# Routing splits and comparisons moved from VectorE to GpSimd, with new dates, in a clustered-attention and MLP kernel

## The chip, the cores and the metric

The kernel runs on one core of one Trainium2 chip. The metric is the device time of one execution in microseconds (us). Before the change three runs gave 298.3, 299.58 and 299.75 us; the median is 299.58 us. The profile is of one execution, taken by the hardware profiler; its times are counted from the first instruction of that execution.

The engines are named as in the profile: PE (TensorE, with its weight loads as PEld), DVE (VectorE), ACT (ScalarE), POOL (GpSimd), SP (SyncE, which here only issues transfers).

## The reference

Inputs are `q`, `k`, `v` of 4 batches x 8 heads x 768 positions x 64 numbers, 16 centroids for each head, and the two weight matrices of an MLP (512 to 2048 and back), all in 32-bit floats.

```python
q_assign = argmax(q_n . c_n)         # q, k and centroids normalised; the nearest of 16 centroids
k_assign = argmax(k_n . c_n)
mask = q_assign[:, :, :, None] == k_assign[:, :, None, :]
scores = where(mask, (q . k) / 8, -1e9)
attn = softmax(scores);  x = attn @ v    # heads side by side: 3072 tokens x 512
h = x @ w_in;  out = (h * sigmoid(h)) @ w_out
```

A position attends only to positions routed to the same centroid. The routing must pick the same centroid as 32-bit arithmetic does, while the matrix products take 16-bit floats.

## The kernel before, in words

**Splits and routing jobs.** A job covers the rows of a few 128-position pieces of `q` and `k`: `k0` to `k7`, `x0`, `x1` for batch 0, and `h8` to `h31`, one for each head of batches 1 to 3. A job goes through these steps:

1. its rows are loaded into a buffer `raw` by a DMA from SP's queue (`load`, L111);
2. `hi` (L123, L125, L127 for ACT, POOL, DVE) writes the upper 16-bit part of 128 times the rows, and `lo` (L132, always DVE) what is left of them, side by side into `hl`;
3. a DMA transposition on SP's queue brings both into `ab` (`xpose`, L141);
4. TensorE multiplies with the normalised centroids (`logits_n`, L180), DVE adds the two parts (`lsum`, L192, into `L`, two buffers), takes the row maximum (`mx_n`, L208) and compares with it (`ge_n`, L217), which gives a one where the centroid is the nearest;
5. the ones become codes: for `h16` to `h31` (the *late* jobs, batches 2 and 3) POOL scales them by 16384 and for the key half subtracts 16384 (`c_scale`, L224 and L225, in `od`, three buffers), SP's queue transposes them (`c_xpose`, L233), and POOL's queue moves them into rows 64 to 79 of `ab` (`c_move`, L237). The earlier jobs go through TensorE (L246), an eviction (L257 or L259) and SP's queue (L261).

With 64 rows of data and 16 rows of codes in `ab`, one product gives the scaled score plus a large number only where the centroids agree, so that the exponential of all others is zero. Where `ab` holds the lower part before, the codes overwrite it.

**Attention.** The work on scores is cut into 192 units of two products each (`qk_mm`, L354); ACT takes the exponentials (`exp`, L359). For every pair of heads and half of the positions TensorE multiplies with the values (`pv`, L371), whose 16-bit copies POOL makes (`cast_v`, L295); DVE divides by the sums (`norm`, L381, L383), and the result is transposed by a DMA or by TensorE.

**MLP.** For each of four batches and two halves there are 16 pieces of the first layer (`unit_a`, L421; tanh on ACT, L441; gate on DVE, L444) and pieces of the second (`part_b`, L480, or `Pair`, L561, seven products of half size for eight, with sums on DVE, L544).

**What sets the order.** Nothing is scheduled by the compiler: each engine runs its instructions in the order in which the code emits them. Up to the 27th exponential the order is a written list (`plan`). Behind it a planner follows: it keeps a clock for each engine and lanes of waiting pieces with assumed times, always takes the piece that can start first, and emits it. `date(p, f)` starts a step when score unit `p` is emitted. `SPLIT` has the unit at which each of h8 to h31 begins its split; `AHEAD`, `VALUES` and `CAST` (one number for each of batches 1 to 3) place its row load, the load of its values and their cast against that. `chain` (L869 and on) books the steps of a job one after another: `split`, `turned`, `landed`, `sums`, `top`, `codes`, `moved`, `known`. `either` (L857) gives a piece to ACT only if ACT is free earlier than DVE by `MARGIN`. `options` chooses TensorE's next piece; the pace of the score units comes from `PACE`, `LEAST`, `LESS` and `GAIN` and the stock of MLP pieces still to do; `HOLD`, `ROUND`, `SIDE` and `LEAD` weigh MLP pieces against each other and against the scores. A score whose codes the planner does not expect yet is not emitted; other work comes first. A row buffer or `hl` buffer of a late chain passes from a job to the one three jobs on.

TensorE's outputs lie in four banks of PSUM for everything but the scores (which have two buffers of two banks); a bank is handed on when its reader is done. `EARLY_T` is the unit from which DVE prepares differences of the second layer's weights for `Pair`.

## Time and profile before

| | us |
|---|---|
| median of three runs | 299.58 |
| lowest and highest run | 298.3, 299.75 |
| the profiled execution, first to last instruction (span) | 297.1 |
| PE busy | 288.0 |
| ACT busy | 221.7 |
| DVE busy | 219.7 |
| POOL busy | 72.3 |

The page gives the profiled execution's span and no other time for it; the runs' times include what lies around the span. Busy time counts instructions on the engine, without waits, semaphores and the issuing of transfers. A matmul's drawn end is modelled, so that neighbouring ones overlap. Each wait is put down to the event that ended it. The granted clock of TensorE was 1.00 throughout.

### The profile page before, as it was taken

How to read it: one execution, taken by the hardware profiler on the slowest of the kernel's cores; microseconds unless marked ns; L12 is line 12 of the kernel's file. 1: busy time of each engine (PE TensorE's matmuls, PEld its weight loads, DVE VectorE, ACT ScalarE, POOL GpSimd, SP SyncE). 2: the span in 40 equal slices, each digit the busy share in tenths (PEclk: the TensorE clock that was granted, in tenths of full speed). 3: DMA queues.
4: the chain of work that ended last, by engine and by line, in shares of the span. 5: the costliest groups of instructions: out<-in, count | busy, mean ns of one | idle time of the engine just before them, and what ended most of it. 6: DMA issues, size and time to landing. Idle time of an engine off the chain costs nothing.

```text
span 297.1 us, 8186 instructions
## 1 busy us (share of the span) xinstructions
PE 288.0 (97%) x3273; PEld 203.4 (68%) x3273; DVE 219.7 (74%) x459; ACT 221.7 (75%) x365; POOL 72.3 (24%) x133
## 2 busy tenths in 40 slices
PE   7899799999999999999999999999999999999995
PEld 3786666566766566667766776678767786767783
DVE  5998559586897799997797766997664553569743
ACT  5899689765896579988579668997798879845410
POOL 2889510001031023544232560243200000000000
PEclk9999999999999999999999999999999999999999
DMA  6689999999866599999877979785220020110113
GB/s 208 206 244 204 158 257 228 170 235 185 242 128 174 133 214 227 209 223 196 232 175 144 196 215 226 170 126 119 74 57 17 13 86 15 49 38 0 35 38 141
DMA packets 77220, 44.61 MB, mean 150 GB/s; under 512 B 56288, under 2 KB 73088, under 8 KB 77184
## 3 DMA queue, kind: packets, MB, share of 16 engines
q1 hardware_dynamic: 71952, 35.55, 51.7%
q0 software_dynamic: 4800, 8.13, 15.0%
q8 instruction: 25, 0.41, 0.6%
q10 hardware_dynamic: 432, 0.43, 0.4%
q14 instruction: 11, 0.09, 0.1%
HBM read 27.30 MB, written 6.29 MB: 113 GB/s over the span
## 4 chain that ended last, share of the span: by engine, by line
PE 85%; DMA 7%; POOL 2%; DVE 2%; issue 1%; ACT 1%; SPq 0%; POOLq 0%; DVEq 0%; ACTq 0%
PE ph L421 28%; PE pS L354 18%; PE po L561 16%; PE pO L371 10%; PE po L480 9%; DMA raw<-in_q_dram 3%; PE psN L180 3%; DMA ab<-cd 3%; DMA ab<-cdt 1%; POOL hl L125 1%; DVE hl L132 1%; DVE ab L166 1%; POOL vt L295 1%; POOL win_s L613 0%; PE px L393 0%
## 5 line engine op out<-in xcount | busy, mean ns | idle before, releaser
L359 ACT ACTIVATE P<-pS 128x768 f16<-128x768 f32 x192 | 156.9, 826 | 36.9 <-PE pS L354 36.0
L421 PE MATMUL ph<-xt,win_s 128*128 128x384 f16 x512 | 97.6, 326 | 0.0
L354 PE MATMUL pS<-ab 128*128 128x384 f16 x384 | 93.2, 326 | 2.2 <-DMA ab<-cd 1.5
L444 DVE SCALAR_TENSOR_TENSOR gt<-tn,ph 128x384 f16<-128x384 f32 x110 | 58.7, 550 | 21.0 <-ACT tn L441 20.4
L421 PEld LDWEIGHTS <-win_s 128*128 128x128 f16 x512 | 49.3, 98 | 31.1
L441 ACT ACTIVATE tn<-ph 128x384 f32<-128x384 f32 x110 | 55.1, 514 | 3.3 <-PE ph L421 2.4
L354 PEld LDWEIGHTS <-ab 128*128 128x128 f16 x384 | 34.5, 98 | 20.8 <-issue 2.5
L371 PEld LDWEIGHTS <-P 128*128 128x128 f16 x1152 | 39.7, 97 | 5.0 <-DVE ab L166 0.9
L371 PE MATMUL pO<-vt,P 128*128 128x65 f16 x1152 | 41.2, 193 | 0.3 <-DVE ab L166 0.3
L132 DVE SCALAR_TENSOR_TENSOR hl<-raw,hl 128x768 f16<-128x768 f32 (+3 forms) x35 | 32.8, 939 | 1.2 <-POOL hl L125 0.5
L561 PEld LDWEIGHTS <-gt 128*128 128x128 f16 x304 | 29.3, 98 | 5.9 <-DVE gt L544 0.4
L480 PE MATMUL po<-wout_s,gt 128*128 128x512 f16 x128 | 32.5, 379 | 0.0
L295 POOL CAST vt<-vn 128x384 f16<-128x384 f32 x32 | 18.8, 598 | 56.2 <-DMA vn<-in_v_dram 40.7
L561 PE MATMUL po<-wout_s,gt 128*128 128x256 f16 x192 | 24.4, 273 | 0.0
L224 POOL TENSOR_SCALAR od<-od 128x96 f16<-128x96 f16 x16 | 9.3, 580 | 53.3 <-DVE od L217 53.2
L381 DVE RECIPROCAL zr<-pO 128x6 f32<-128x6 f32 x32 | 6.2, 193 | 18.9 <-PE pO L371 18.8
L180 PEld LDWEIGHTS <-ab 128*128 128x128 f16 x458 | 17.3, 97 | 4.0 <-DVE ab L166 0.3
L480 PEld LDWEIGHTS <-gt 128*128 128x128 f16 x128 | 12.0, 98 | 10.6
L383 DVE TENSOR_TENSOR xn<-pO,zr 128x384 f16<-128x384 f32 x32 | 17.8, 557 | 1.1
L180 PE MATMUL psN<-stk,ab 128*128 128x32 f16 (+1 forms) x458 | 18.6, 188 | 0.0
L561 PE MATMUL po<-tw,sg 128*128 128x256 f16 x128 | 16.3, 273 | 0.0
L192 DVE TENSOR_REDUCE L<-psN 128x192 f32<-128x384 f32 (+1 forms) x27 | 14.8, 549 | 1.9 <-PE psN L180 1.7
(101 smaller groups left out, 259.0 us busy)
## 6 DMA issues: line engine op xcount, KB each, us to landing
raw<-in_k_dram SPq DMA_DIRECT2D x31, 192.0 KB, 4.0
out_dram<-ot SPq DMA_DIRECT2D x23, 256.0 KB, 2.4
raw<-in_q_dram SPq DMA_DIRECT2D x24, 192.0 KB, 3.9
vn<-in_v_dram SPq DMA_DIRECT2D x16, 192.0 KB, 4.2
vn<-in_v_dram POOLq DMA_DIRECT2D x16, 192.0 KB, 4.3
win_s<-in_moe_w_in_dram POOLq DMA_DIRECT2D x8, 256.0 KB, 6.2
wout_s<-in_moe_w_out_dram POOLq DMA_DIRECT2D x4, 512.0 KB, 18.8
raw<-in_q_dram SPq DMA_DIRECT2D x2, 384.0 KB, 4.2
```

The lines of the kernel that those rows point to most:

```text
L132: nc.vector.scalar_tensor_tensor(out=hl[:, s, 1, :], in0=raws[job.name][:, s, :], scalar=QS, in1=hl[:, s, 0, :], op0=ALU.mult, op1=ALU.sub ...
L180: nc.tensor.matmul(L[:, n % g, :, n // g], ab[:, i, :], stk[:, job.groups[i // 3][0], x : x + w], start=(x == 0), stop=(x + w == 2 * HC),)
L295: nc.gpsimd.tensor_copy(vt[:, :, 0:D], vns.pop(i))
L354: nc.tensor.matmul(pS[:, e, 0:HALF], abs_[kj.name][:, kn, :], rhs, start=True, stop=True)
L359: nc.scalar.activation(out=P, in_=pst.pop(u)[:, :, 0:HALF], func=AF.Exp, bias=0.0, scale=ESC)
L371: nc.tensor.matmul(o[:, (2 * t + h) * VW : (2 * t + h + 1) * VW], Ps[i + h, c, j // 2][:, j % 2, ts(t, 128)], vtb[(i + h) % 13][:, j, 0:VW ...
L383: nc.vector.tensor_tensor(out=xn, in0=ov[:, :, 0:D], in1=zr.unsqueeze(2).to_broadcast([128, 2 * NM, D]), op=ALU.mult)
L421: nc.tensor.matmul(ph[:, 0:HALF], win_s[:, r, ts(fb, 128)], xts[b, c][:, r, :], start=(r == 0), stop=(r == NR - 1))
L441: nc.scalar.activation(out=tn, in_=ph[:, 0:HALF], func=AF.Tanh, bias=0.0, scale=1.0)
L444: nc.vector.scalar_tensor_tensor(out=gt[:, fb, :], in0=tn, scalar=1.0, in1=ph[:, 0:HALF], op0=ALU.add, op1=ALU.mult)
L480: nc.tensor.matmul(po, gts[b, c][:, fc, ts(t, 128)], wout_s[:, fc, :], start=(fc == 0), stop=(fc == NFB - 1))
L561: nc.tensor.matmul(o, l[:, f, :], x, start=(f == 0 and k in begins), stop=(f == HK - 1), skip_group_check=True)
```

## The change

Three things, all in the planner's part:

- For ten jobs (`BY_GP`) the upper split `hi` runs on POOL; before, `either` gave it to DVE or ACT. The planner books 2.5 us for it. The lower split stays on DVE behind it.
- For the late jobs the comparison is taken apart: POOL subtracts the row maximum from the sums, in place in `L`, and `c_scale` compares the difference with zero and scales in the same instruction. Equality with the maximum gives zero, so the ones stay where they were. DVE's comparison of these jobs goes. The planner books 0.8 us on POOL.
- The constants of the planner's pace, the dates of all splits, loads, value loads and casts are others.

```diff
     def ge_n(job):
...
-        nc.vector.tensor_tensor(
-            out=ohv(job), in0=Ls.pop(job.name), in1=mx.unsqueeze(2).to_broadcast([128, g, HC, m]), op=ALU.is_ge
-        )
+        mx = mx.unsqueeze(2).to_broadcast([128, g, HC, m])
+        if job.late:
+            nc.gpsimd.tensor_tensor(out=Ls[job.name], in0=Ls[job.name], in1=mx, op=ALU.subtract)
+        else:
+            nc.vector.tensor_tensor(out=ohv(job), in0=Ls.pop(job.name), in1=mx, op=ALU.is_ge)

     def c_scale(job):
-        o = ohv(job)
-        nc.gpsimd.tensor_scalar(out=o[:, :, :, 0:3], in0=o[:, :, :, 0:3], scalar1=OHV, scalar2=None, op0=ALU.mult)
-        nc.gpsimd.tensor_scalar(
-            out=o[:, :, :, 3:6], in0=o[:, :, :, 3:6], scalar1=OHV, scalar2=-OHV, op0=ALU.mult, op1=ALU.add
-        )
+        o, d = ohv(job), Ls.pop(job.name)
+        nc.gpsimd.tensor_scalar(out=o[:, :, :, 0:3], in0=d[:, :, :, 0:3], scalar1=0.0, scalar2=OHV, op0=ALU.is_ge, op1=ALU.mult)
+        nc.gpsimd.tensor_scalar(out=o[:, :, :, 3:6], in0=d[:, :, :, 3:6], scalar1=0.0, scalar2=-OHV, op0=ALU.is_lt, op1=ALU.mult)
...
-    PACE, LEAST, LESS, GAIN = 1.37, 23, 13, 0.03
-    HOLD, ROUND, SIDE, LEAD = -7, 8, 4, 11
+    PACE, LEAST, LESS, GAIN = 1.33, 36, 11, 0.035
+    HOLD, ROUND, SIDE, LEAD = -9, 9, 3, 13
...
-    MARGIN = 0.1
-    EARLY_T = 67
+    BY_GP = [10, 13, 16, 22, 24, 25, 27, 28, 29, 31]
+    MARGIN = 0.5
+    EARLY_T = 62
...
-            either(t, 0.5, 0.72, lambda e: hi(job, "act" if e == "A" else None), lambda t: add("DVE", t, 0.9, lambda: lo(job), turned, 1.5), 1.5)
+            def lower(t):
+                add("DVE", t, 0.95 if i in BY_GP else 0.9, lambda: lo(job), turned, 1.5)
+
+            i = int(job.name[1:])
+            if i in BY_GP:
+                add("POOL", t, 2.5, lambda: hi(job, "pool"), lower, 1.5)
+            else:
+                either(t, 0.5, 0.72, lambda e: hi(job, "act" if e == "A" else None), lower, 1.5)
...
-            add("DVE", t, 0.33, lambda: ge_n(job), codes, 0.6)
+            if job.late:
+                add("POOL", t + 0.06, 0.8, lambda: ge_n(job), codes, 0.2)
+            else:
+                add("DVE", t, 0.33, lambda: ge_n(job), codes, 0.6)
...
-    SPLIT = [27, 27, 33, 41, 43, 44, 51, 56, 67, 72, 79, 80, 81, 83, 84, 87, 99, 102, 105, 122, 124, 132, 135, 142]
-    AHEAD, VALUES, CAST = [9, 8, 10], [1, 0, 4], [7, 3, 12]
+    SPLIT = [25, 26, 29, 38, 39, 49, 53, 57, 61, 68, 74, 77, 72, 76, 86, 77, 68, 90, 92, 123, 117, 114, 123, 126]
+    AHEAD, VALUES, CAST = [7, 8, 7], [0, 1, 3], [12, 4, 14]
```

## The prediction

> **What bounds the kernel now.** I read the table of busy time by stage first, cut into the written list (to 45 us), the planner's stretch (45 to 285) and the end. Columns: stretch, its length, then busy us of PE, PEld, DVE, ACT, POOL, the granted clock, DMA share, GB/s.
>
> ```profile
> 0.00:15.00 15.00, 11.93 (x159) 7.73 (x160) 11.68 (x43) 10.47 (x20) 7.96 (x16) 1.00 0.68 206
> 15.00:30.00 15.00, 14.68 (x260) 11.40 (x258) 13.22 (x33) 14.45 (x24) 13.35 (x19) 1.00 0.98 224
> 30.00:45.00 15.00, 13.24 (x156) 9.08 (x154) 9.01 (x22) 11.53 (x21) 4.81 (x9) 1.00 1.07 210
> 45.00:165.00 120.00, 120.00 (x1357) 80.07 (x1356) 101.30 (x204) 94.69 (x157) 29.14 (x58) 1.00 0.93 194
> 165.00:180.00 15.00, 14.79 (x173) 10.99 (x172) 9.75 (x19) 10.25 (x14) 7.27 (x14) 1.00 0.84 213
> 180.00:285.00 105.00, 105.00 (x1108) 77.14 (x1106) 70.38 (x134) 79.57 (x132) 9.80 (x20) 1.00 0.32 72
> 285.00:297.10 12.10, 8.40 (x76) 6.96 (x73) 4.35 (x9) 0.77 (x2) 0.00 (x0) 1.00 0.24 87
> ```
>
> PE is drawn idle for 9.05 us of 297.1, and where it is idle decides this case. 3.07 + 0.32 + 1.76 = 5.15 us lie in the written list, whose order, loads and engines the edit leaves alone (its jobs are neither late nor among the ten). 3.70 us lie after 285, and this is why:
>
> ```profile
> 293.43 0.38 ACT L604 ACTIVATE ot<-po 128x256 f32<-128x256 f32 x1 [4.11 <-PE po L561]
> 293.85 0.35 ACTq L605 DMA_DIRECT2D out_dram<-ot  x1
> ```
>
> The last product is evicted and written out after TensorE is done; that order is fixed, and the clock is 1.00 already. In the 240 us that the edit reorders, PE is idle 0.21 us. The matmuls themselves stay the same in number and shape. So DVE work taken away is worth nothing by itself: it has to remove a PE wait, and hardly one is left.
>
> The chain of waits shows that one, the timeline its neighbours:
>
> ```profile
> 161.72 0.79 issue
> 162.50 4.39 DMA ab<-cdt
> ```
> ```profile
> 158.94 0.55 POOL L237 DMA_DIRECT2D ab<-cdt  x1 [3.27 <-PE ph L421]
> 162.40 0.49 PE L354 MATMUL pS<-ab 128*128 128x384 f16 x2
> 162.50 0.52 POOL L237 DMA_DIRECT2D ab<-cdt  x1 [2.49 <-PE pS L354]
> 166.94 0.50 PE L354 MATMUL pS<-ab 128*128 128x384 f16 x2 [0.21 <-DMA ab<-cdt]
> ```
> ```profile
> ab<-cdt POOLq DMA_DIRECT2D x16, 48.0 KB, 3.6
> ...
> ab<-cd SPq DMA_DIRECT2D x10, 48.0 KB, 2.5
> ```
>
> Moves run in job order; these are the seventh and eighth of sixteen, for h22 and h23. Counting pairs of scores, 162.40 is unit 114, the first that needs h22's codes, and 166.94 is unit 117, the first that needs h23's. By the median 3.6 us to landing, h22's codes arrive at 162.5, just as they are used; h23's arrive 4.4 us after 162.50 and PE waits. So this run stands at the edge in two neighbouring jobs, and a landing that varies by a microsecond shows as time. The weights of that second score are drawn later than the matmul wait alone, and a matmul's drawn end can cover up to 0.16 us of idle time (326 ns drawn, four units in 0.65), so I price the wait at 0.4 us.
>
> **The change part by part.**
>
> ```profile
> L127 DVE TENSOR_SCALAR hl<-raw 128x768 f16<-128x768 f32 x21 | 11.7, 562 | 0.0
> L217 DVE TENSOR_TENSOR od<-L,mxn 128x192 f16<-128x192 f32 x16 | 6.0, 376 | 0.4
> L224 POOL TENSOR_SCALAR od<-od 128x96 f16<-128x96 f16 x16 | 9.3, 580 | 53.3 <-DVE od L217 53.2
> L225 POOL TENSOR_SCALAR od<-od 128x96 f16<-128x96 f16 x16 | 6.4, 401 | 0.0
> L125 POOL TENSOR_SCALAR hl<-raw 128x768 f16<-128x768 f32 x2 | 4.3, 2128 | 1.4 <-DMA raw<-in_q_dram 1.4
> L655 POOL TENSOR_TENSOR cy<-cs,hf 128x1 f32<-128x1 f32 x1 | 0.6, 572 | 1.8 <-DVE cs L653 1.8
> ```
>
> *Ten upper splits.* DVE does 21 of the planner's 24 now (ACT the rest) and loses 10 x 0.56 = 5.6 us; POOL gains 10 x 2.13 = 21.3 us. Each of the ten chains becomes 2.13 - 0.56 = 1.57 us longer. The planner books 2.5 us, 0.37 above the row.
>
> *Sixteen comparisons.* DVE loses 6.0 us. POOL gains a subtraction of two f32 tensors, 128x192, which the trace does not show. Nearest rows: the POOL split takes 2.77 ns an element, 0.53 us for 192, and twice that, 1.06, if two inputs are read in turn; the one two-input row, 0.57 us for one element, is nearly all overhead and lies between. I take the planner's 0.8 as their middle: 12.8 us, bounds 8.5 to 17. The Trainium skill (GPSIMD Engine Reference, 3.1 Elementwise) gives 4497 ns for 2048 elements of such an addition, so an estimate of 0.42 us, and 6.7 us for sixteen; no run here shows it yet.
>
> *Comparison with zero and scaling.* Still two POOL instructions of 96 elements, now from f32: 0.58 + 0.40; by the split's 2.77 ns an element they would take 0.27 each, 0.4 less in sum, and as much more is my bound above; I count no change. A late job's chain to its codes grows by 0.8 - 0.38 = 0.4 us.
>
> In sum POOL goes from 72.3 to 72.3 + 21.3 + 12.8 = 106.4 us, far from a bound; DVE loses 11.6. Neither is on PE's path. What covers DVE's lateness already: 120 us of PE without a gap while DVE is busy 101.3.
>
> *Sharing between POOL and DVE.* A POOL split beside DVE's lower split has rows in the written list, and a POOL cast beside DVE's comparison has rows later:
>
> ```profile
> 7.46 3.42 POOL L125 TENSOR_SCALAR hl<-raw 128x576 f16<-128x576 f32 x2 [3.18 <-DMA raw<-in_q_dram]
> 12.16 3.52 POOL L125 TENSOR_SCALAR hl<-raw 128x576 f16<-128x576 f32 x2 [1.27 <-PE pTq L155]
> 118.86 0.52 POOL L295 CAST vt<-vn 128x384 f16<-128x384 f32 x1
> ```
> ```profile
> 6.43 0.76 DVE L132 SCALAR_TENSOR_TENSOR hl<-raw,hl 128x576 f16<-128x576 f32 x1
> 7.57 1.16 DVE L132 SCALAR_TENSOR_TENSOR hl<-raw,hl 128x576 f16<-128x576 f32 x1
> 14.65 0.75 DVE L132 SCALAR_TENSOR_TENSOR hl<-raw,hl 128x576 f16<-128x576 f32 x1
> 118.95 0.73 DVE L217 TENSOR_TENSOR od<-L,mxn 128x192 f16<-128x192 f32 x1
> ```
>
> Alone the lower split takes 0.76 us; started 0.11 us after a POOL split it takes 1.16, and in the middle of one 0.75. So a POOL split costs DVE 0 to 0.4 us: 0 to 4 us for ten, less than the 11.6 it gives. The comparison behind the cast waited until the cast's end (0.73 against a mean of 0.38).
>
> The Trainium skill (SBUF — State Buffer, SBUF: two separate sides) says that the port pair shared by DVE and GpSimd is locked for a whole instruction and the other one fully blocks. The cast agrees; the split does not: by the rule 14.65 would have ended after 15.68 + 0.75, and it ended at 15.40. The rule's result is a rival below.
>
> *New dates.* For h16 to h23 the split dates go from 67, 72, 79, 80, 81, 83, 84, 87 to 61, 68, 74, 77, 72, 76, 86, 77; the last three jobs' go from 132, 135, 142 to 114 (h29), 123, 126. The two rows that give the pace are the code move and the first score (unit 63) of h13:
>
> ```profile
> 83.89 0.60 SPq L261 DMA_DIRECT2D ab<-cd  x1
> 92.36 0.49 PE L354 MATMUL pS<-ab 128*128 128x384 f16 x2
> ```
>
> From 92.36 to 166.94 there are 54 units, 1.38 us each. Buffers pass from job to job three apart (chains of h16, h19, h22 and h17, h20, h23), so the earlier heads of the chains bring the tails too. The first five of these jobs move by 3 to 9 units; I count 4 to 6, 5 to 8 us, against 1.6 (split) + 0.4 (codes) given back per link, twice in a chain. h23's codes should come 2 to 5 us earlier, and the 0.4 us go. With them go the lateness of others in runs where DMA lands later. Of each moved step the load, the transposition and the code move shift together on SP's and POOL's queues; no DMA is added. The pacing constants only say which PE piece comes when; with PE full they move nothing unless the stock of MoE pieces runs dry.
>
> **The sum.** 297.1 - 0.4 = 296.7 for an execution like the profiled one. The median of the runs, 299.58, lies 2.5 us above that span (launch, and whatever that run waited more), and the three runs spread from 298.3 to 299.75. So the excess over the lowest, 1.3 us, is waiting that comes and goes; the code landings at the edge are one place for it. I take a quarter of it, 0.3. 299.58 - 0.4 - 0.3 = **298.9**.
>
> **The rivals.**
>
> *All of the scatter was late codes.* Then 1.3 + 0.4 go: 297.9. For it: two jobs at the edge. Against: the list's 1.76 us around DMA landings at 30 to 45 can vary just as well, and it stays.
>
> *DVE stands behind POOL (slower).* The lower split is next in DVE's order and now waits for POOL, whose order is fixed too and waits for landings:
>
> ```profile
> 118.31 0.56 POOL L237 DMA_DIRECT2D ab<-cdt  x1 [4.91 <-PE ph L421]
> 156.64 0.81 PE L421 MATMUL ph<-xt,win_s 128*128 128x384 f16 x4
> 157.63 0.51 ACT L441 ACTIVATE tn<-ph 128x384 f32<-128x384 f32 x1
> 158.18 0.55 DVE L444 SCALAR_TENSOR_TENSOR gt<-tn,ph 128x384 f16<-128x384 f32 x1 [0.53 <-ACT tn L441]
> ```
> ```profile
> 45.77 0.65 PE ph L421 x4
> 46.75 0.65 PE ph L421 x4
> ```
>
> A split behind a move that lands late is late by as much; behind the waiting lower split stand the gates, and PE waits for the gates' banks. A bank is held 158.73 - 156.64 = 2.1 us, a unit starts every 0.98; with one of the four banks held by an open product, three turn in 2.94, so 0.85 us is covered. It decides where POOL runs over 0.85 us later than booked. If four of ten splits run 2 us late: 4 x 1.15 = 4.6, 298.9 + 4.6 = 303.5. Against: one to two us of wobble in DVE (the 1.16 and 0.73 above) reached PE nowhere after 45 us.
>
> *The lock holds.* If each split blocked DVE's next two-input instruction for half its 2.13 us and half of the ten hit the gates uncovered in full: 10 x 1.06 x 0.5 = 5.3, so 304.2. Against: the row 14.65.
>
> *Batch 1 comes too late.* h13 to h15 go from 44, 51, 56 to 49, 53, 57, and h13's split goes to POOL. Five units are 6.9 us, the split 1.6; the slack is 92.36 - 83.89 less 2.5 to land, 6.0. Short by 2.5 us, 301.4, if nothing in the chain was waiting for something else and the planner had booked it otherwise (it places a score only when it expects the codes).
>
> *It does nothing:* the stall stays or moves, 299.6; within the forecast's own range.
>
> **Chances.** Forecast with the last case 0.53; scatter 0.25; DVE behind POOL 0.12; lock 0.04; batch 1 0.06. About 0.5% (1.5 us) is what a measurement of this kernel tells from no change: faster 0.25 (297.9), same 0.53, slower 0.22. The range: from 297.2, the scatter's case less four such gaps of 0.16 us under drawn ends, up to 302.0, past batch 1, which leaves out the two dearest, 0.16. The forecast's own range is 298 to 300.5.
>
> **What would show it.** Right: PE still busy 240 of 240 us between 45 and 285; no score waiting for a code landing; POOL near 106 us, DVE near 208 to 212; POOL's subtraction 0.5 to 1.1 us. Wrong: a wait of DVE's lower split for POOL's upper one over 1 us with a PE gap behind it; scores near unit 63 waiting for codes; the end after the last matmul longer than 3.9 us; or a gain past 1.7 us, which could only come from the written list or from matmuls that run faster.

## The result

The changed kernel takes 302.04 us by the median of eight runs (300.76 to 306.98); eight runs of the kernel before took 299.53 (298.3 to 300.18). The ratio is 1.0104 with a 95% interval of 1.0066 to 1.0142: about 3.1 us slower, where the forecast was 0.7 us faster. The profiled execution took 302.1 us, 1.8 us more than its span of 300.3. The medians themselves lie 2.5 us apart. Ratios leave out every run more than 1.5% above the fastest of its own kernel, some of them at the full granted clock, among them six of the ten with only the splits undone and three of the ten with the idle subtractions; medians hold all runs.

The table of stages of the changed kernel, cut as for before (stretch, length, busy us of PE, PEld, DVE, ACT, POOL, granted clock, DMA share, GB/s):

```profile
0.00:15.00 15.00, 12.33 (x164) 8.12 (x165) 11.71 (x43) 10.66 (x20) 8.60 (x16) 1.00 0.66 206
15.00:30.00 15.00, 14.49 (x254) 11.17 (x251) 13.19 (x33) 14.45 (x23) 10.73 (x14) 1.00 0.96 223
30.00:45.00 15.00, 14.74 (x168) 9.88 (x165) 10.58 (x24) 13.16 (x24) 5.76 (x11) 1.00 1.02 216
45.00:165.00 120.00, 116.96 (x1334) 77.62 (x1331) 94.62 (x184) 92.76 (x150) 57.96 (x80) 1.00 0.97 200
165.00:180.00 15.00, 13.92 (x165) 10.45 (x166) 10.57 (x18) 11.07 (x17) 13.03 (x15) 1.00 0.62 154
180.00:285.00 105.00, 104.65 (x1097) 76.13 (x1096) 66.29 (x123) 77.26 (x127) 15.82 (x25) 1.00 0.32 72
285.00:300.30 15.30, 11.94 (x107) 10.04 (x105) 7.43 (x15) 2.43 (x6) 0.00 (x0) 1.00 0.19 69
```

PE's idle time in the planner's 240 us went from 0.21 to 3.04 + 1.08 + 0.35 = 4.47 us. In the written list, whose instructions are the same, it fell from 5.15 to 3.44; at the end it went from 3.70 to 3.36. So 2.2 us of the 3.2 by which the span grew are drawn idle time, and 1.0 is drawn busy time: PE's total went from 288.0 to 289.0 with the same matmuls. A drawn end that covers the first part of a gap would do that: six gaps at the 0.16 us that the prediction worked out for one are 1.0 us.

PE's gaps in that stretch, from the timeline (start, length, engine, line, what, idle before and what ended it):

```profile
50.66 0.34 PE L393 MATMUL px<-ident,xn 128*128 128x128 f16 x3 [0.93 <-DVE xn L383]
...
117.04 0.81 PE L421 MATMUL ph<-xt,win_s 128*128 128x384 f16 x4 [0.23 <-DVE gt L444]
...
119.31 0.81 PE L421 MATMUL ph<-xt,win_s 128*128 128x384 f16 x4 [0.78 <-DVE gt L444]
...
126.46 0.52 PE L180 MATMUL psN<-stk,ab 128*128 128x32 f16 x12 [1.02 <-DMA ab<-hl]
...
166.08 0.50 PE L354 MATMUL pS<-ab 128*128 128x384 f16 x2 [1.15 <-DMA ab<-cdt]
...
193.52 0.65 PE L371 MATMUL pO<-vt,P 128*128 128x65 f16 x16 [0.35 <-DVE gt L444]
```

They sum to 4.46 us, nearly all of the 4.47, in five places (117.04 and 119.31 are one). All of this is one execution.

**50.66.** The chain of waits, then the timeline:

```profile
36.56 8.49 DMA raw<-in_k_dram
```
```profile
45.22 0.95 DVE L132 SCALAR_TENSOR_TENSOR hl<-raw,hl 128x768 f16<-128x768 f32 x1
...
45.24 2.92 POOL L125 TENSOR_SCALAR hl<-raw 128x768 f16<-128x768 f32 x1 [9.13 <-PE ph L421]
...
48.19 1.25 DVE L132 SCALAR_TENSOR_TENSOR hl<-raw,hl 128x768 f16<-128x768 f32 x1 [1.09 <-POOL hl L125]
...
50.04 0.56 DVE L383 TENSOR_TENSOR xn<-pO,zr 128x384 f16<-128x384 f32 x1
```

h10's rows need 8.49 us to land (45.05; the timeline names a PE product as the last event before the split, the chain names this landing). Its date went from unit 33 to 29, while its rows are loaded in the written list as before; the planner takes the rows of h8 to h11 as there from its start (`loaded[f"h{n}"] = 0.0`), so nothing in it warns of the landing. POOL's split begins only at 45.24 and takes 2.92 us beside DVE's lower split of h9. DVE's lower split of h10, next in its order, stands for 1.09 us, and the quotient at 50.04, for which PE waits 0.93 us, stands behind it. With the old dates and both moves on POOL (the run that is replanned below) POOL's split begins at 44.80, and the quotient (48.01) stands ahead of the lower split (50.89). Nor does the gap come each time: in the changed kernel with one load held back, which is the same up to 72 us, the rows land at 45.26, POOL's split takes 2.49 us and PE has no such gap.

**117.04 and 119.31.** DVE's and POOL's timelines:

```profile
113.97 2.55 DVE L132 SCALAR_TENSOR_TENSOR hl<-raw,hl 128x768 f16<-128x768 f32 x1
...
118.71 1.00 DVE L444 SCALAR_TENSOR_TENSOR gt<-tn,ph 128x384 f16<-128x384 f32 x2
```
```profile
114.22 0.52 POOL L295 CAST vt<-vn 128x384 f16<-128x384 f32 x1
114.69 0.57 POOL L219 TENSOR_TENSOR L<-L,mxn 128x192 f32<-128x192 f32 x1
115.19 0.51 POOL L295 CAST vt<-vn 128x384 f16<-128x384 f32 x1
115.67 1.31 POOL L226 TENSOR_SCALAR od<-L 128x96 f16<-128x96 f32 x1
```

While POOL has four short instructions in a row, among them the new subtraction and the new scaling, one lower split of DVE lasts 2.55 us (the mean before was 0.99), and the gates behind it come late (the last two begin at 118.71).

**126.46.** SP's queue: the transposition for h19 (second row) stands behind that of an attention result, which takes 2.54 us to issue; it goes out at 121.40, and PE waits 1.02 us for it, until it has landed (126.41).

```profile
118.81 2.54 SPq L412 DMA_TRANSPOSE xt<-xn  x1
121.40 1.48 SPq L141 DMA_TRANSPOSE ab<-hl  x1
```

Late is relative: in the kernel before, the same transposition went out at 118.88, took 7.5 us and also landed at 126.41, and nothing waited, since its product came only at 128.06. After the change PE is ready for it at 125.44.

```profile
118.88 2.37 SPq L141 DMA_TRANSPOSE ab<-hl  x1
...
128.06 0.51 PE L180 MATMUL psN<-stk,ab 128*128 128x32 f16 x12
```

**166.08.** h23's code move, the one stall that the forecast saw, is still there and larger:

```profile
161.53 0.57 POOL L237 DMA_DIRECT2D ab<-cdt  x1 [2.43 <-DMA cdt<-od]
```

It is issued at 161.53 instead of 162.50, 1.0 us earlier, but its first use was due at 164.93 (166.08 less the wait) instead of 166.73, 1.8 us earlier, and the wait grew from 0.21 to 1.15 us.

**193.52.** DVE waited 0.63 us for a POOL split and 1.01 us for a row load just before:

```profile
188.70 1.31 DVE L132 SCALAR_TENSOR_TENSOR hl<-raw,hl 128x768 f16<-128x768 f32 x1 [0.63 <-POOL hl L125]
191.02 0.81 DVE L127 TENSOR_SCALAR hl<-raw 128x768 f16<-128x768 f32 x1 [1.01 <-DMA raw<-in_k_dram]
```

The groups by line and shape (busy us, mean ns, idle before and its releasers) give the new durations:

```profile
L132 DVE SCALAR_TENSOR_TENSOR hl<-raw,hl 128x768 f16<-128x768 f32 x26 | 28.5, 1095 | 2.6 <-POOL hl L125 2.5
...
L125 POOL TENSOR_SCALAR hl<-raw 128x768 f16<-128x768 f32 x12 | 27.0, 2246 | 40.5 <-DMA raw<-in_k_dram 21.9 <-PE ph L421 9.1 <-DMA ab<-hl 7.1
...
L219 POOL TENSOR_TENSOR L<-L,mxn 128x192 f32<-128x192 f32 x16 | 11.7, 733 | 22.6 <-DVE mxn L208 22.5
L226 POOL TENSOR_SCALAR od<-L 128x96 f16<-128x96 f32 x16 | 11.2, 700 | 1.0
L227 POOL TENSOR_SCALAR od<-L 128x96 f16<-128x96 f32 x16 | 10.7, 667 | 0.0
```

Before, the same 26 lower splits took 990 ns each:

```profile
L132 DVE SCALAR_TENSOR_TENSOR hl<-raw,hl 128x768 f16<-128x768 f32 x26 | 25.7, 990 | 0.8 <-POOL hl L125 0.5
```

So each stall of this execution has a last event that can be named. What the traces can't say is which part of the change is to blame for them: the engines that were exchanged, or the order in which the planner now emits everything.

### The profile page after: what moved, and what is told of

The parts are those of the page before. It is cut to its first block, busy times and chain, and to the rows that moved or that the text cites. A ratio compares the mean times of both kernels' runs of the same rounds, so it can differ in the third digit from the quotient of the medians.

```text
span 300.3 us, 8172 instructions
## 1 busy us (share of the span) xinstructions
PE 289.0 (96%) x3273; PEld 203.4 (68%) x3273; DVE 214.4 (71%) x434; ACT 221.8 (74%) x362; POOL 111.9 (37%) x159
## 4 chain that ended last, share of the span: by engine, by line
PE 72%; DMA 11%; DVE 7%; POOL 3%; ACT 2%; SPq 2%; issue 2%; POOLq 0%; DVEq 0%; ACTq 0%
PE ph L421 19%; PE po L561 16%; PE pS L354 15%; PE pO L371 9%; PE po L480 9%; DMA raw<-in_k_dram 7%; PE psN L180 3%; POOL hl L125 2%; DVE hl L132 2%; DMA ab<-hl 2%; DMA cdt<-od 2%; ACT P L359 1%; DMA ab<-cdt 1%; DVE gt L444 1%; SPq L111 1%
## 5 line engine op out<-in xcount | busy, mean ns | idle before, releaser
L421 PE MATMUL ph<-xt,win_s 128*128 128x384 f16 x512 | 99.2, 326 | 1.0 <-DVE gt L444 1.0
L441 ACT ACTIVATE tn<-ph 128x384 f32<-128x384 f32 x108 | 53.5, 501 | 6.3 <-PE ph L421 4.9
L125 POOL TENSOR_SCALAR hl<-raw 128x768 f16<-128x768 f32 (+1 forms) x16 | 33.7, 2110 | 44.2 <-DMA raw<-in_k_dram 21.9
L132 DVE SCALAR_TENSOR_TENSOR hl<-raw,hl 128x768 f16<-128x768 f32 (+3 forms) x35 | 35.2, 1011 | 2.9 <-POOL hl L125 2.5
L219 POOL TENSOR_TENSOR L<-L,mxn 128x192 f32<-128x192 f32 x16 | 11.7, 733 | 22.6 <-DVE mxn L208 22.5
L295 POOL CAST vt<-vn 128x384 f16<-128x384 f32 x32 | 18.0, 580 | 4.0 <-DMA vn<-in_v_dram 2.1
L467 ACT ACTIVATE tn<-ph 128x768 f32<-128x768 f32 x10 | 8.1, 811 | 12.8 <-PE ph L421 12.8
```

Source lines behind the costliest of these rows:

```text
L125: nc.gpsimd.tensor_scalar(out=o, in0=i, scalar1=QS, scalar2=None, op0=ALU.mult)
L132: nc.vector.scalar_tensor_tensor(out=hl[:, s, 1, :], in0=raws[job.name][:, s, :], scalar=QS, in1=hl[:, s, 0, :], op0=ALU.mult, op1=ALU.sub ...
L295: nc.gpsimd.tensor_copy(vt[:, :, 0:D], vns.pop(i))
L421: nc.tensor.matmul(ph[:, 0:HALF], win_s[:, r, ts(fb, 128)], xts[b, c][:, r, :], start=(r == 0), stop=(r == NR - 1))
L441: nc.scalar.activation(out=tn, in_=ph[:, 0:HALF], func=AF.Tanh, bias=0.0, scale=1.0)
```

## The experiments

The theories: **the moves** (POOL is slow or late and DVE stands behind it, or the shared port costs), **the order** (the new dates give another sequence on every queue, whatever engine a piece runs on), **the pace** (the eight constants that weigh TensorE's pieces), and later **the value load** (a load on POOL's queue beside a transposition makes the transposition land late). "In the new order" means that the changed kernel's sequence is kept, with its bookings, and only the engine or the instruction at a place is exchanged; "in the old order" the same with the sequence of before. "Replanned" means that the planner made a sequence from the constants named. The runs compute what the kernel before computes, by the same or the exchanged instructions; only one (the idle subtractions) has work added that nothing uses.

**All results.** Ratio to the kernel before, which was timed anew with each group of runs (medians 299.38 to 300.08); PE idle is 240 us less PE's busy time between 45 and 285 in one profiled execution.

| | splits | comparisons | ratio, 95% interval | median, runs | PE idle |
|---|---|---|---|---|---|
| *new order* (changed kernel) | POOL | POOL | 1.0104 [1.0066, 1.0142] | 302.04, 8 | 4.5 |
| | DVE, ACT | POOL | 1.0091 [1.0043, 1.0139] | 305.55, 10 | 5.7 |
| | POOL | DVE | 1.0026 [0.9992, 1.0060] | 299.99, 10 | 2.2 |
| | DVE, ACT | DVE | 1.0132 [1.0058, 1.0207] | 304.93, 4 | 3.4 |
| with idle subtractions on POOL | POOL | DVE | 1.0037 [1.0003, 1.0072] | 301.58, 10 | 4.5 |
| load held | DVE, ACT | DVE | 1.0062 [1.0025, 1.0099] | 300.71, 10 | 1.6 |
| load held | POOL | DVE | 1.0035 [1.0002, 1.0069] | 301.05, 12 | 3.4 |
| load held | POOL | POOL | 1.0106 [1.0047, 1.0166] | 303.05, 4 | 4.8 |
| *old order* | POOL | DVE | 0.9978 [0.9940, 1.0017] | 299.81, 10 | 0.7 |
| again | POOL | DVE | 0.9985 [0.9949, 1.0020] | 299.34, 12 | 1.0 |
| | DVE, ACT | POOL | 0.9982 [0.9945, 1.0020] | 300.08, 10 | 4.2 |
| | POOL | POOL | 1.0154 [1.0103, 1.0204] | 304.57, 6 | 7.2 |
| load early | DVE, ACT | DVE | 1.0020 [0.9984, 1.0055] | 300.71, 10 | 0.3 |
| *replanned* new dates | DVE, ACT | DVE | 1.0216 [1.0147, 1.0286] | 307.6, 4 | 4.2 |
| new dates | POOL | DVE | 1.0075 [1.0029, 1.0120] | 301.81, 10 | 4.2 |
| new dates, old pace | POOL | POOL | 1.0108 [1.0068, 1.0149] | 303.47, 4 | 4.3 |
| old dates, old pace | POOL | POOL | 0.9988 [0.9953, 1.0024] | 299.77, 10 | 1.5 |
| old dates, LEAST 36 | DVE, ACT | DVE | 1.0026 [0.9995, 1.0056] | 300.56, 10 | 1.5 |

The last column is of one execution and the ratio of all, so they needn't agree: the old order with the comparisons on POOL has 4.2 us of idle time in a profiled execution of 302.3 us, while its ten runs are level with before.

### The engines undone in the new order

Ten upper splits back to DVE:

```diff
-                add("POOL", t, 2.5, lambda: hi(job, "pool"), lower, 1.5)
+                add("POOL", t, 2.5, lambda: hi(job), lower, 1.5)
```


> The changed kernel with every instruction emitted in its own order, but the ten upper splits issued on DVE at the place where POOL had them. Theory A (DVE stands behind POOL's slow split, and shares its port): the gaps of PE at 50.4 us (1.1) and 193 us (0.5) go, most of that near 117 us (1.3) too, and the time falls by 2 to 3 us from 302.0, to 299 to 300. Theory B (the new dates and order are what is slow, whichever engine works): it stays at 301.5 to 302.5. Theory C (the comparison on POOL): it stays at 301 to 302.

Measured: 1.0091, and 305.55 us by the median of all ten. Nothing is gained, so it isn't the splits on POOL by themselves that cost. Theory A had the places right: in the profiled execution (307.26 us) the gaps at 50.66, 117 to 119 and 193.52 us are gone, and so is the one at 166. But PE waits for two transpositions there instead, 2.22 us before 76.82 and 2.56 us before 131.07.

The comparison as before (subtraction off, DVE compares, POOL scales):

```diff
-        if job.late:
-            nc.gpsimd.tensor_tensor(out=Ls[job.name], in0=Ls[job.name], in1=mx, op=ALU.subtract)
-        else:
-            nc.vector.tensor_tensor(out=ohv(job), in0=Ls.pop(job.name), in1=mx, op=ALU.is_ge)
+        nc.vector.tensor_tensor(out=ohv(job), in0=Ls.pop(job.name), in1=mx, op=ALU.is_ge)
```
(with `c_scale` as it was.)

> The changed kernel in its own order, but the late jobs' comparison on DVE as before, at the place where POOL had the subtraction, and the scaling as before; the ten splits stay on POOL. Theory A (splits): 301.5 to 302.5, the gap at 50.4 us stays. Theory B (dates and order): 301.5 to 302.5. Theory C (comparison: POOL's runs of short instructions keep DVE's two-input instructions waiting, as the 2.55 us lower split at 114 us, and the codes come later): the gaps at 117, 126 and 166 us go (3.8 us together) and the time is 298.5 to 300.

Measured: 1.0026, PE idle 2.2 us instead of 4.5. Against the changed kernel that is 0.8% less. Of theory C's three places one is free of a gap in the profiled execution, 126 us; 0.54 us are left at 119.17, and h23's codes are late again, by 1.25 us at 164.84. The gap at 50 us isn't there either, although the splits are still on POOL.

Both undone, so that only the sequence differs from before:

```diff
-                add("POOL", t, 2.5, lambda: hi(job, "pool"), lower, 1.5)
+                add("POOL", t, 2.5, lambda: hi(job), lower, 1.5)
...
+        nc.vector.tensor_tensor(out=ohv(job), in0=Ls.pop(job.name), in1=mx, op=ALU.is_ge)
```

> The changed kernel's order and dates with both edits undone: splits and comparison are on DVE, each at the place in the emission where POOL had it. Theories A and C (POOL's work is what costs): 298.5 to 300, as before the change. Theory B (dates and order): 301.5 to 302.5. If both count, between.

Measured: 1.0132 [1.0058, 1.0207], 4.0 us, from four runs. With each piece on its old engine and of its old duration, the new sequence is slower than before, and no faster than the whole change. But it was planned for the durations on POOL, and none of the changed kernel's five gaps is in its profile. Of its 3.4 us of idle time 3.24 are one gap that no theory had:

```profile
69.81 1.90 SPq L141 DMA_TRANSPOSE ab<-hl  x1
70.04 0.55 POOL L290 DMA_DIRECT2D vn<-in_v_dram  x1
78.95 0.52 PE L180 MATMUL psN<-stk,ab 128*128 128x32 f16 x12 [3.24 <-DMA ab<-hl]
```

A transposition issued at 69.81 lands 9.1 us later, and PE stands for 3.24 us.

The new dates with everything else as before, replanned:

```diff
-    BY_GP = [10, 13, 16, 22, 24, 25, 27, 28, 29, 31]
+    BY_GP = []
```
(and `ge_n`, `c_scale` and `top` of before.)

> The planner plans anew with the new dates and constants, but without the two moves to POOL. Theories A and C: 298.5 to 300. Theory B: 301.5 to 302.5, with the wait for h10's row load (split date 29 instead of 33) still in front of a PE gap near 50 us.

Measured: 1.0216. It agrees with the run above, with a reservation: without the bookings on POOL the planner itself already expects 2.9 us of gaps on PE (0.1 in the kernel before, 0.0 in the changed one), so this plan is worse than the one under test by the planner's own clock. That clock is a poor judge, though: it expects 1.8 us of gaps in the run with the old dates and both moves (0.9988 below), and none in the changed kernel.

### The engines moved in the old order

```diff
-lambda e: hi(job, "act" if e == "A" else None)
+lambda e: hi(job, "pool" if int(job.name[1:]) in BY_GP else "act" if e == "A" else None)
```
(with the list `BY_GP` written out.)

> The kernel before, every instruction in its old place, but the ten upper splits issued on POOL. The runs so far have the splits on POOL as a gain in the new order (300.0 with them and the comparison on DVE, 304.9 with both on DVE). Theory A (a split on POOL is good wherever it is, because DVE then doesn't stand waiting for a row load): 298 to 299.4. Theory D (it is good only in the new order, which books 2.5 us for it; in the old order, which booked 0.5, DVE's lower split stands behind POOL): 301 to 304, with waits of DVE's lower split for POOL's upper one of 1 to 2 us, ten of them, and PE gaps behind some.

The comparisons alone, in the kernel before:

```diff
-        nc.vector.tensor_tensor(out=ohv(job), in0=Ls.pop(job.name), in1=..., op=ALU.is_ge)
+        if job.late:
+            nc.gpsimd.tensor_tensor(out=Ls[job.name], in0=Ls[job.name], in1=mx, op=ALU.subtract)
...
```
(and `c_scale` of the changed kernel.)

> The kernel before in its old order, but the late jobs' comparison on POOL by subtraction and comparison with zero. Theory C (the comparison on POOL costs about 2 us by itself, by the port it shares with DVE): 301 to 302, lower splits of DVE stretched past 1.5 us beside POOL's instructions. Theory E (it costs only where codes are late already): 299.4 to 300.4, gaps at units 114 to 117 alone, about 1 us.

Both, replanned with the bookings of the changed kernel and the old dates and constants (also `HOLD` to `LEAD`, `MARGIN`, `EARLY_T`, `AHEAD`, `VALUES` and `CAST`, which the cut leaves out):

```diff
-    PACE, LEAST, LESS, GAIN = 1.33, 36, 11, 0.035
+    PACE, LEAST, LESS, GAIN = 1.37, 23, 13, 0.03
...
-    SPLIT = [25, 26, 29, 38, 39, 49, 53, 57, 61, 68, 74, 77, 72, 76, 86, 77, 68, 90, 92, 123, 117, 114, 123, 126]
+    SPLIT = [27, 27, 33, 41, 43, 44, 51, 56, 67, 72, 79, 80, 81, 83, 84, 87, 99, 102, 105, 122, 124, 132, 135, 142]
```


> Both moves to POOL, planned anew with the dates and constants of before. Theory B (the new dates cost, the moves do not): 298.5 to 299.9. Theory C (comparison costs 2 us wherever it is): 300.5 to 302. If the planner's booking of 2.5 us keeps DVE from standing behind POOL, no wait of the lower split over 1 us.

Measured: 0.9978 with the splits, 0.9982 with the comparisons, 0.9988 with both. All three intervals hold 1. The stage of the first one:

```profile
45.00:285.00 240.00, 239.34 (x2630) 167.74 (x2629) 176.68 (x344) 182.52 (x298) 68.31 (x103) 1.00 0.66 141
```

DVE is down from 181.44 to 176.68 here and PE is still full. The price of zero that the forecast set on each move holds in this order. The run with both is the plainest comparison of the case: the changed kernel has the same moves with the same bookings and differs in the dates and constants alone, and it is at 1.0104. In the run with the splits alone DVE's lower split even waits more for POOL than in the changed kernel (2.5 us there; time in total, times, longest):

```profile
DVE hl L132 <- POOL hl L125: 3.6, 4, 1.6
```

and nothing comes of it: a wait of DVE for POOL costs only where something due soon stands behind it.

Both moves in the old order without any booking for them:

```diff
-lambda e: hi(job, "act" if e == "A" else None)
+lambda e: hi(job, "pool" if int(job.name[1:]) in BY_GP else "act" if e == "A" else None)
...
+            nc.gpsimd.tensor_tensor(out=Ls[job.name], in0=Ls[job.name], in1=mx, op=ALU.subtract)
```


> The kernel before in its old order with both moves to POOL at the old places. Each alone changed nothing (0.998 of before, each with an interval of 0.4%). If the two add without touching PE: 0.996 to 1.000. If POOL becomes crowded between 100 and 200 us: 1.003 to 1.008, with DVE's lower split waiting for POOL's upper one. It could beat both kernels.

Measured: 1.0154, from six runs. Here the forecast's slower rival appears in full, in the profiled execution, which is the longest of the six (309.58 us; how long the wait is in the others, no trace shows). POOL's, DVE's and PE's timelines:

```profile
134.30 0.50 POOL L295 CAST vt<-vn 128x384 f16<-128x384 f32 x1 [2.48 <-DMA vn<-in_v_dram]
...
136.06 2.16 POOL L125 TENSOR_SCALAR hl<-raw 128x768 f16<-128x768 f32 x1
```
```profile
138.25 1.04 DVE L132 SCALAR_TENSOR_TENSOR hl<-raw,hl 128x768 f16<-128x768 f32 x1 [5.62 <-POOL hl L125]
```
```profile
141.46 1.89 PE L561 MATMUL po<-wout_s,gt 128*128 128x256 f16 x8 [4.38 <-DVE xn L383]
```

POOL waits for a value load, the split behind it begins late, DVE stands for 5.62 us, and PE for 4.38. Each move alone costs nothing in this order, both together do: in these rows the split stands behind the cast, and between the two POOL has a code move and one of the new subtractions. A plan that books both (0.9988 above) pays nothing.

### New dates with one part each

```diff
-            if job.late:
-                add("POOL", t + 0.06, 0.8, lambda: ge_n(job), codes, 0.2)
...
+            add("DVE", t, 0.33, lambda: ge_n(job), codes, 0.6)
```
(and `ge_n`, `c_scale` of before, replanned.)

> The new dates and constants and the ten splits on POOL, planned anew, the comparison on DVE as the planner books it. By the run with the comparison put back in the changed order (300.0): 299.2 to 300.5. Theory B alone (dates): 301.5 to 305.

```diff
-    PACE, LEAST, LESS, GAIN = 1.33, 36, 11, 0.035
-    HOLD, ROUND, SIDE, LEAD = -9, 9, 3, 13
+    PACE, LEAST, LESS, GAIN = 1.37, 23, 13, 0.03
+    HOLD, ROUND, SIDE, LEAD = -7, 8, 4, 11
```


> The changed kernel with the old constants of the pace (PACE, LEAST, LESS, GAIN, HOLD, ROUND, SIDE, LEAD), planned anew; both moves and the new dates stay. Theory P (the faster pace of the scores moves the uses of the transposed rows and codes towards their landings and takes the margin that the earlier dates give): 299.3 to 300.5, unit 117 near 167 to 169 us and h23's codes waiting for it, not it for them. Theory Q (the dates of the splits are at fault: h10's split before its rows have landed, loads of batch 1 between the transpositions): 301.5 to 302.5, with the gaps near 50 and 75 us.

Measured: 1.0075 without the comparison, in a plan that expects no gap at all, and 1.0108 with the whole change at the old pace. The pace constants of the change are not the cause. What is left between this run and the one with the old dates (0.9988) are the dates (`SPLIT`, `AHEAD`, `VALUES`, `CAST`) and with them `MARGIN` and `EARLY_T`, which were not varied by themselves. The second plan expects 0.65 us of gaps of its own; 1.08%, 3.2 us, is about five times that.

The pace in the other direction, in the kernel before:

```diff
-    PACE, LEAST, LESS, GAIN = 1.37, 23, 13, 0.03
+    PACE, LEAST, LESS, GAIN = 1.37, 36, 13, 0.03
```


> The kernel before with LEAST 36 instead of 23, planned anew: the scores end about 4 us earlier by the planner's clock, nothing else is changed. Theory P: 300.5 to 302. Theory Q: 299.2 to 300.2.

Measured: 1.0026 [0.9995, 1.0056], not to be told from nothing.

### Is it the port?

To the new order with the comparison on DVE (1.0026), sixteen subtractions of zeros on POOL are added, each behind the scaling of a late job, with the shapes of the real ones and results that nothing reads:

```diff
+            nc.gpsimd.tensor_tensor(out=jv, in0=jv, in1=jm, op=ALU.subtract)
```


> The changed order with the comparison back on DVE (300.0), and in addition sixteen subtractions of 128x192 zeros on POOL, each right behind a late job's scaling, used by nothing (work added, result unchanged). Theory C1 (the port that POOL and DVE share makes the comparison on POOL dear): 301.3 to 302.3. Theory C2 (it is the codes' longer way through POOL, or DVE's order behind it): 299.6 to 300.6.

Measured: 1.0037 [1.0003, 1.0072] against 1.0026 for the same kernel without them and 1.0104 for the changed one. By the middle values POOL's added work as such, and its use of the port, is worth 0.1 of the 0.8% that the comparison's move costs; the intervals would allow 0.6. By the medians of all ten runs it is more: 301.58 us, 1.6 above before, where the run without the subtractions was 0.6 above. And the profiled execution, the longest of the ten (304.35 us), has 4.5 us of idle time on PE, with gaps at 120.86 (0.54), 128.27 (1.28), 168.20 (1.44) and 195.77 us (0.47), near the changed kernel's. So POOL's added work is not cleared. The other candidate is where the real subtraction stands: in the chain to the codes, which now come out of POOL's queue behind whatever POOL does first. These runs don't decide between them.

### Is it the value load?

In the kernels whose profiles were compared up to here, the transposition that PE waits for at 74 to 79 us (h12's) landed after 4.4 to 4.9 us with the old dates (first value load on POOL's queue at 85 to 87 us), after 5.4 to 6.7 with the new dates and splits on POOL (load at 73 to 74), and after 7.1 to 9.1 with the new dates and splits on DVE (load at 69 to 70, in the same microsecond). That suggested the load as the cause. It was held back by one cast (h16's values, on POOL):

```diff
-lambda: load_v(i, nc.gpsimd), lambda t: got_v(i, t)
+lambda: load_held(i), lambda t: got_v(i, t)
```
(`load_held` keeps the load of 16 until the next cast.)

> The new order with both moves undone, and POOL's load of h16's values issued one cast later (near 81 us instead of 69.8). Theory V (that load stretches h12's transposition): it lands within 4.4 to 5.5 us, the gap of PE near 78 us (3.4) is under 0.6, and the time falls from 304.9 to 300 to 302.5. Rival W (DMA is simply full there): landing 7 to 9 us, 304 to 306.

The same edit, of which this is the other line, on the kernel with the comparison back, and on the changed kernel itself:

```diff
-            cast_v(i), done_)
+            cast_held(i), done_)
```
(`cast_held` sends the held load out behind the cast.)

> The changed order with the comparison back on DVE (300.0) and the load held back by one cast. Theory V: the landing goes from 5.4 to below 5 us and 0.2 to 0.5 us are gained, 299.3 to 300. Rival W: 299.8 to 300.5.

> The changed kernel with the load held back by one cast. Theory V: little, since POOL's split of h13 holds it back to 72.7 us already: 301.3 to 302.3; the waits near 50, 117, 126, 166 and 193 us stay. Rival W: 301.5 to 302.5.

With both engines undone the ratio came down from 1.0132 [1.0058, 1.0207] to 1.0062 [1.0025, 1.0099] (the intervals overlap), and the gap is gone:

```profile
66.96 1.96 SPq L141 DMA_TRANSPOSE ab<-hl  x1
...
73.58 0.51 PE L180 MATMUL psN<-stk,ab 128*128 128x32 f16 x12
...
76.10 0.55 POOL L290 DMA_DIRECT2D vn<-in_v_dram  x1
```

But in this run the transposition was also issued 2.9 us earlier, and it still took 6.3 us with no such load near. On the kernel with the comparison back the hold gave nothing (1.0035 against 1.0026), on the changed one neither (1.0106 against 1.0104): the changed kernel's gaps at 119, 126, 166 and 194 us stay where they were. Against expectation, the one near 50 us isn't in that execution.

The mirror of it: in the kernel before, the same load is issued early, right beside transpositions.

```diff
+        if len(casts) == 4:
+            vns[16] = mp.tile([128, NJ, D], f32, name="vn", tag="sg0", bufs=1)
+            nc.gpsimd.dma_start(...)
```


> The kernel before, its order kept, but h16's values are loaded by POOL right behind its fourth cast of the planner's part, near 70 us instead of 85, into a buffer that is free there. Theory V: h12's or h13's transposition (issued at 70 and 72 us) takes 6.5 to 9 us to land, PE waits 1 to 3 us near 76 to 78 us, and the time is 300.8 to 303. Rival W: both land within 5.5 us, 299.3 to 300.3.

Measured: 1.0020 [0.9984, 1.0055]; the load went out at 72.31 us and h12's transposition at 72.36, the two transpositions took 5.9 and 5.1 us, and PE waited for neither. So this run didn't bring the 9.1 us back. All traces together speak for the load more than these runs do: from h11's on, 80 transpositions were issued from 1.5 us before a value load to 1 us behind one, and landed after a median of 5.6 us; the other 319 after 4.5. The five that took over 8 us, three of them in the old order, are all among the 80. That is a coincidence in time and not a cause shown; and the load explains a part of one control kernel at best, and nothing of the changed one, which is no faster with the load held.

### The best version once more

The splits alone in the old order had the lowest ratio, and were run again:

```diff
-lambda e: hi(job, "act" if e == "A" else None)
+lambda e: hi(job, "pool" if int(job.name[1:]) in BY_GP else "act" if e == "A" else None)
```

> The kernel before in its old order with the ten splits on POOL, timed again in more rounds, as the one version so far that might beat both kernels. If the splits are worth something where the order leaves room: 0.994 to 0.997 of before. If they are worth nothing, as the forecast's term of zero says: 0.998 to 1.002.

Measured: 0.9985 [0.9949, 1.0020]. Two sets of runs below one, neither apart from it: no version here beats the kernel before by an amount that can be measured.

## Why the prediction was wrong

**DVE work taken away "is worth nothing by itself": right.** DVE fell from 219.7 to 214.4 us and nothing came of it; in the old order 4.8 us less on DVE gave a ratio of 0.998 with an interval that holds 1.

**No cost for the moves to POOL: right in the old order for each move, and for both together in a plan that has the old dates** (0.9978, 0.9982, 0.9988). For both together it was right for a reason that the forecast gave only in part: the planner placed the work around the longer chains. Without that it is false (1.0154), and in the new order the comparison's move costs 0.8%.

**The durations.** Splits: 2246 ns measured, 2128 taken. Subtraction: 733, 0.8 us taken, bounds 0.53 to 1.06. Scaling: "I count no change" at 0.58 + 0.40 us; measured 0.70 + 0.67, 0.39 more each time and just inside the bound of 0.4. POOL came to 111.9 us instead of 106.4; the scaling alone is 6.2 us over, the splits 1.4, subtractions and casts are under. DVE was forecast at 208 to 212 and stayed at 214.4. Its 26 lower splits took 1095 ns instead of 990, 2.8 us in sum, inside the forecast's 0 to 4 us of sharing; and it went from 21 upper splits to 12, not to 11, since one of the ten was on ACT before. The rest is spread over many small groups.

**"New dates": the step that failed.** It stood in the sum with -0.4 us for h23's wait and -0.3 for lateness elsewhere, and no term for harm. Measured, with both moves made and planned for, the new dates and constants stand at 1.0104 and the old ones at 0.9988; with the engines as before the new sequence costs 1.3% [0.6, 2.1], and 0.62% [0.25, 0.99] when the load beside its one long landing is held back. In the trace PE's idle time in the stretch rose from 0.21 to 4.47 us, and h23's wait, which was to go, grew to 1.15. Three errors lie in it:

- *Heads for tails.* "The earlier heads of the chains bring the tails too": h16's split did move, from 99.69 to 87.54, but h23's did not. The upper split runs at 133.65 on ACT before and at 134.37 on DVE after, the lower one at 135.85 and 137.94.

```profile
133.65 0.84 ACT L123 ACTIVATE hl<-raw 128x768 f16<-128x768 f32 x1
```
```profile
87.54 2.13 POOL L125 TENSOR_SCALAR hl<-raw 128x768 f16<-128x768 f32 x1 [7.13 <-DMA ab<-hl]
...
134.37 0.55 DVE L127 TENSOR_SCALAR hl<-raw 128x768 f16<-128x768 f32 x1
```

  Between them stand the buffers: POOL waits 7.13 us at the head for a transposition (h14's, two jobs back and not the three that the forecast counted; it landed at 87.35) that must land before the split may write. An earlier date there buys a place in the queue and not an earlier start. h23's codes were sent 1.0 us earlier and landed 0.9 us earlier, not 2 to 5, and their score was due 1.8 us earlier itself.

- *Only the dates of one chain were followed.* I looked for what came earlier, and only for h13 to h15 for what might come late. The gap at 50.66 is h10's: a date four units earlier (a unit starts every 0.98 us there, by the forecast's rows at 45.77 and 46.75) put the lower split ahead of a quotient that PE needs, for rows that take 8.49 us to land. Every moved date changes which instruction stands ahead of which on five queues; that was priced at zero.

- *"One to two us of wobble in DVE (the 1.16 and 0.73 above) reached PE nowhere after 45 us."* The rows show less: 1.16 is 0.40 above the 0.76 alone, and lies at 7.57 us, and 0.73 is 0.35 above the mean. So they say nothing of a lateness of a microsecond. That the old sequence can take one, the runs in the old order show (1.6 us of waiting for POOL, no gap behind it). In the new one a wait of 1.09 us stood before a gap of 0.93, and the split of 2.55 us before 0.23 + 0.78.

**The rival "DVE stands behind POOL" had the mechanism and not the cause.** The lower split's waits for POOL (below: total, times, longest) stood before the gaps at 50.66 and, with a row load, at 193.52, 0.93 + 0.35 us of the 4.46. Its threshold of 0.85 us isn't borne out: it was worked out for gates, while PE waited for a quotient at 50.66, and a wait of 1.6 us in the old order led to no gap.

```profile
DVE hl L132 <- POOL hl L125: 2.5, 4, 1.1
```

Its price of 4.6 us assumed four waits of 2 us each; they were four, but 2.5 us in sum. The other 3.2 us of gaps come from DVE slowed beside POOL's short instructions, from a transposition and from h23's codes, whose uses moved further forward than they did. "The lock holds" was priced on the splits; they were level with before in the old order. "Batch 1 comes too late" didn't happen: no gap before 100 us is a score's.

**The base.** The median "lies 2.5 us above that span (launch, and whatever that run waited more)": the time outside the span is 1.8 us in every run here, so the profiled execution of before took 298.9, 0.7 below the median that the forecast started from. The 0.3 us hoped for from the scatter is a quarter of another difference, the 1.3 us from the lowest run to the median; no run shows that late codes make it up.

**What remains open.** Which of the 24 dates does it can't be said, nor what share `MARGIN` and `EARLY_T` have, which changed along with them. Plans with part of the new dates weren't run. Nor is it shown why the new order with both moves undone is slower than with the splits on POOL (1.0132 against 1.0026, the intervals overlap by a hair). The trace gives one place, the landing of 9.1 us; why it took so long isn't settled. That the comparison's move costs 0.8% in the new order is measured twice (1.0104 against 1.0026, and 1.0106 against 1.0035 with the held load); whether the longer chain or POOL's added work does it is open, as the chain itself wasn't varied. The gaps differ from trace to trace in one order, so a share of the loss can't be given to each.

## What to carry to other kernels

In a kernel whose every engine follows a fixed sequence, a change of that sequence is the change: it can cost more than any instruction that is moved, and it has no row in the profile of before to price it by, so its range must reach to both sides by what a single late landing can do (here 1 to 3 us). Test an exchange of engines in the old sequence and the new sequence with the old engines, each alone, and both exchanges planned with the old dates, before judging the whole; here the first and the last are worth nothing and the second costs 0.6 to 1.3%. A plan without gaps on its own clock is no promise: the one that expected none lost 1%, and one that expected 1.8 us of them lost nothing. And a wait of an engine is to be priced by what stands behind it and how soon that is due: in the profiled executions 1.6 us of waiting cost nothing in one sequence, 1.09 went with a gap of 0.93 in another, and 5.62 with 4.38.

## What the runs showed of the hardware

**A gap of 2.2 us was enough to halve the clock.** With the splits back on DVE in the new order, a gap on PE ended so:

```profile
76.82 0.52 PE L180 MATMUL psN<-stk,ab 128*128 128x32 f16 x12 [2.22 <-DMA ab<-hl]
...
77.50 2.54 PE L421 MATMUL ph<-xt,win_s 128*128 128x384 f16 x8
```

and the table of stages for the 5 us behind it shows PE as busy all the time at a mean granted clock of 0.66:

```profile
77.00:82.00 5.00, 5.00 (x33) 2.73 (x30) 3.11 (x7) 2.94 (x5) 0.84 (x2) 0.66 1.15 295
```

In slices of half a microsecond the granted clock is 0.50 from 78.0 to 81.0 us; a mean of 0.66 over 5 us is then 3.4 us at half clock, and 1.7 us of work lost. A second gap of that run, 2.56 us before 131.07, did the same. The same eight matmuls take 1.46 us with both engines undone, behind the longer gap of 3.24 us that didn't touch the clock:

```profile
79.63 1.46 PE L421 MATMUL ph<-xt,win_s 128*128 128x384 f16 x8
```

The Trainium skill (TensorE: Matmul & The Clock Gate, Part 1: The HAM clock gate) has the clock fall after at least one idle window of about 3.4 us that runs freely, not started by the gap. The 3.4 us at half clock agree with the window's length; a fall after 2.2 us of drawn idle time (a drawn end can hide some more, 0.16 us by the prediction's estimate) is earlier than the rule's words allow, and the spared gap of 3.24 us fits a window that doesn't start with it. That kernel's ten runs spread from 300.6 to 310.9 us. Four of them have a mean clock of 0.988 to 0.994 (the profiled one, with its two falls, 0.989); the other six have 1.000 and still spread from 300.6 to 306.4, so the clock makes only a part of the spread.

**POOL and DVE hold each other up, and it matters which starts first.** At 45.22 us (rows above) DVE's lower split began just before POOL's upper one: DVE's took its usual 0.95 us, POOL's 2.92 instead of 2.13. At 175.51 POOL began first:

```profile
175.51 2.14 POOL L125 TENSOR_SCALAR hl<-raw 128x768 f16<-128x768 f32 x1
...
175.72 1.45 DVE L132 SCALAR_TENSOR_TENSOR hl<-raw,hl 128x768 f16<-128x768 f32 x1
```

POOL's took its usual time, and DVE's 0.5 us more than usual, but DVE's ended 0.48 us before POOL's. In the row of short POOL instructions (113.97) the lower split ended at 116.52, 0.95 us after 115.57, which is about the end of the third (115.70), and the fourth took 1.31 us. The Trainium skill (SBUF — State Buffer, SBUF: two separate sides) has the first of the two take the shared ports for its whole instruction. The row at 45.22 and the short instructions fit that within 0.15 us; the row at 175.51 doesn't, as DVE would have ended after 177.65. So a POOL split costs DVE's lower split half a microsecond there, and rows of short instructions, to which the comparison's move adds one, up to 1.6. The mean of a lower split rose by only 0.1 us, though 12 POOL splits of 2.25 us lay around.

**POOL's scaling got longer.** With the comparison in it and from f32 it takes 0.70 and 0.67 us for 96 elements, from f16 and without it 0.58 and 0.40. The source's type and the operations changed together, so which of the two does it isn't shown.
